# Windowed attention feeding a squared-ReLU FFN on one core: block sums of a batch gathered into one visit, and the scores of a visit's two groups in one run

## The chip, the cores and the metric

The kernel runs on one core of one Trainium2 chip. The metric is device time in microseconds, the median of three runs. Engines are named as in the profile: PE is TensorE (PEld its weight loads), DVE VectorE, ACT ScalarE, POOL GpSimd, SP the queue that issues all DMAs here.

## What is computed

Attention over 4 batches of 8 heads, 768 positions and 64 dimensions, in which a query sees the keys nearer than 16 positions and, besides, one summary of each block of 32 positions: the maximum of the block's keys and the mean of its values. The attention's output, 3072 tokens of 512, goes through a two-layer FFN.

```python
k_sum = k.reshape(B, H, nb, block, D).max(axis=3)      # block = 32, nb = 24
v_sum = v.reshape(B, H, nb, block, D).mean(axis=3)
scores_l = scale * q @ k.T                             # kept where |i - j| < 16
scores_s = scale * q @ k_sum.T + log(block)
a = softmax(concat([masked scores_l, scores_s]))
x = a @ concat([v, v_sum])                             # 3072 x 512
out = relu(x @ w_in) ** 2 @ w_out                      # 512 -> 2048 -> 512
```

## The kernel before

**Groups.** Queries are taken in 48 groups of 64, 12 to a batch, all heads at once. A group sees 118 key columns: 24 block maxima and 94 neighbours. The keys of a batch lie in one SBUF tile `kb`, whose first 24 columns are the block maxima (`batch_k`: loads KL, maxima KM on DVE). So that a group's 118 columns are contiguous, the 24 maxima are copied along `kb` to stand just ahead of the window (`move`, task KC, on POOL).

**Block means of the values** (`batch_v`) are matmuls against a constant matrix: 768 rows of values are loaded in six DMAs (FV), three tasks (VM) of 16 small matmuls each (24x128 outputs) add them up in one PSUM buffer `vps`, and VS copies it to SBUF, from where three groups of each batch fetch it (LS). From batch 1 on the loaded values lie in the three buffers `t`, which the weight conversion and the output copies use too.

**The FFN** works on units of 8 groups (512 tokens) and 16 slices of the inner dimension. FI is 12 matmuls of 128x512 into a PSUM buffer `h`, RL, SQ, GH and GL on ACT and DVE make the squared ReLU in two parts, FO is 12 matmuls of 128x512 (6 each at a unit's first and last slices). Weights are loaded raw (WL) and converted in the first 115 us (WM, WH on ACT, WR, WJ, WW on DVE). There are 2 buffers `h`; FI, the value products and the block means share them.

**A visit** (`visit`, from group 10 on one for each pair of groups) puts attention work between two FFN items of PE. V11 is the visit that multiplies the values of groups 10 and 11 and makes the scores of 12 and 13. Before, `products` emits the 16 score matmuls of the first group, then `move` on POOL, then the 32 value matmuls of the earlier pair, then the 16 score matmuls of the second group, which need what POOL moved. 19 visits, V9 to V45, do all of this; V47 has values alone. Softmax (M, X, E, R, N, T on DVE and ACT) and a transposition through DRAM (TW, TR) lie between a group's scores and its values.

**Order.** `Plan.order` runs a list of tasks through a small model of costs, keys and buffers and so fixes the order of each engine's instructions; each engine then executes in that order. The means' tasks are keyed some 28 us ahead of their batch.

Of the kernel before, what the change touches and what calls it, by code (L numbers as in the profile page):

```python
# [42 lines left out]
ONE_EXP = 1  # L43
NPE = 8
LAG = 2
HALVED = 2


# [4 lines left out]
def first_key(w, S):  # L53
    return min(max(TQ * w - WINDOW + 1, 0), S - LOC)
# [140 lines left out]
def attention_then_relu2_ffn(  # L195
# [75 lines left out]


    places = [f"w{f}" for f in reversed(range(SINGLE, NF))]

    def lend(name, *shapes):
        b = buf(places.pop(0), 1, (P, 4 * DM), F32, f"{name}_lent")
# [145 lines left out]
    t_means = add("means", "POOL", 1.0, make_means, -88)  # L422

    def batch_v(b):
        key = wanted(b * NW) - 28 if b else -60
        out_ps = h_buf(f"vps{b}")
        vs = vs_bufs[b] = buf("vs", 1, (NB, DM), F32, f"vs{b}")
        last = None
        for i in range(0, S // P, 2):
            if b:  # L430
                x = buf("t", 3, (P, 2 * DM), F32, f"fv{b}_{i}")
                xs = [Part(x, 0, DM), Part(x, DM, 2 * DM)]
            else:
                x, xs = first_v[i], first_v[i : i + 2]
            loads = []
            for k in range(2):
                new = not k and (b or i % 4 == 0)
                loads.append(add(
                    f"FV{b}_{i + k}", "SP", 0.45,
                    lambda i=i + k, x=xs[k]: nc.sync.dma_start(out=x.tile, in_=vS[b, i * P : (i + 1) * P, :]),  # L440
                    key - 4 + i + k, behind=None if new else t, take=[x] * bool(new), use=[x] * (not new),
                    size=4 * P * DM, begin=key - 10 if b else 0, late=LATE if b else 0,
                ))
# [15 lines left out]

        def gather():  # L460
            for c in range(NSQ):
                copy(out=vs.tile[:, c * P : (c + 1) * P], in_=out_ps.tile[c * SQ : c * SQ + NB, :P])

        copy = nc.scalar.copy if b else nc.vector.tensor_copy
        t_VS[b] = [add(f"VS{b}", "ACT" if b else "DVE", 1.1, gather, key + 7, [last], take=[vs], use=[out_ps])]


    t_QL, s_bufs = {}, {}
# [1 line left out]
    def loads(g):  # L470

        b, w = divmod(g, NW)
        k0 = first_key(w, S)
        due = wanted(g)
        q, vv = q_bufs[g], v_bufs[g]
        early = g < EARLY
        lq = t_QL[g] = add(
            f"QL{g}", "SP", 0.45, lambda: nc.sync.dma_start(out=q.tile, in_=qW[g]), due - (26 if early else 50), take=[q],
            size=2 * P * DM, begin=due - (45 if early else 65),
        )  # L480

        def load_v():
            if g < vF.shape[0]:

                nc.sync.dma_start(out=vv.tile, in_=vF[g])
                return

            for r0, r1 in ((0, 96),) if k0 + 96 <= S else ((0, 64), (64, LOC)):
                nc.sync.dma_start(out=vv.tile[NB + r0 : NB + r1, :], in_=vS[b, k0 + r0 : k0 + r1, :])

        def load_s():
            nc.sync.dma_start(out=vv.tile[:NB, :], in_=vs_bufs[b].tile)  # L492

        def copy_s():
            nc.gpsimd.tensor_copy(out=vv.tile[:NB, :], in_=vs_bufs[b].tile)
# [5 lines left out]
        if g < EARLY or w < NV or (b == 0 and g < EARLY + NV):  # L501
            ts = t_VS[b]
            if g >= COPIED:
                key = FIRST_LS + g if early else due - 19
                lv.append(add(f"LS{g}", "SP", 0.45, load_s, key, ts + lv, use=[vv, vs_bufs[b]], size=4 * NB * DM))
            else:
                lv.append(add(f"LS{g}", "POOL", 0.62, copy_s, due - 8, ts + lv, use=[vv, vs_bufs[b]]))

    def mask_of(g):
        w = g % NW  # L510
        off = first_key(w, S) - TQ * w
        return masks[off], t_mask[off]
# [26 lines left out]

    def move(g):  # L540

        k0, nxt = (first_key(w, S) for w in (g % NW, g % NW + 1))
        nc.gpsimd.tensor_copy(out=kb[:, :, nxt : nxt + NB], in_=kb[:, :, k0 : k0 + NB])  # L543

    def keys_of(g, pairs):

# [3 lines left out]
    def first_attention(g):  # L550


        loads(g)
        due = wanted(g)
        parts = [(0, 1), (2, 3)] if g == 0 else [range(NPAIR)]
        by_pe = g < PE_MASKS
        s_bufs[g] = [o_buf(f"s{g}_{i}") for i in range(len(parts))]
        t_S[g] = []
        for i, pairs in enumerate(parts):
            t_S[g].append(add(  # L560
                f"S{g}_{i}", "PE", (1.1 if by_pe else 0.6) / len(parts), lambda i=i, pairs=pairs: scores(g, pairs, by_pe, i),
                due - 15, keys_of(g, pairs) + [t_unscale, mask_of(g)[1]] * by_pe, take=[s_bufs[g][i]], use=[q_bufs[g]],
            ))
        softmax(g, by_pe)
# [160 lines left out]
                    rhs=av[:KEYS, 2 * c : 2 * c + 2, j, :], start=True, stop=True,  # L725
                )

    def visit(both, then=()):

        n, g = len(both), both[-1]  # L730
        due = wanted(g)
# [7 lines left out]
        use = [a_bufs[g] for g in both] + [v_bufs[g] for g in both]  # L739
        if g >= RING:  # L740
            deps.append(t_FI[(g - RING) // UG, NF - 1])
        if then:
            s = s_buf(f"s{then[0]}")
            for g in then:
                loads(g)
                s_bufs[g] = [s]
            deps += keys_of(then[0], range(NPAIR)) + [t_QL[then[1]]] + [t_T[g] for g in both]
            use += [q_bufs[g] for g in then]
# [11 lines left out]
        t_v = add(  # L760
            f"V{both[-1]}", "PE", 0.65 * n + 0.6 * len(then), products, due, deps, take=[x_ps] + [s] * bool(s), use=use
        )
# [210 lines left out]
    def groups(n):  # L973

        nonlocal done_g
        while done_g < n:
            g = done_g
            if g and g % NW == 0:
                batch_k(g // NW)
                batch_v(g // NW)  # L980
            if g < FIRST_S:
                first_attention(g)
                if g < UG:
                    visit([g])
                done_g += 1
            else:
                visit([g - 2, g - 1], [g, g + 1])
# [79 lines left out]
```

## Time and profile before

| | |
|---|---|
| median of 3 runs | 621.16 us (620.18 to 621.87) |
| the profiled execution | 620.11 us, its span 618.4 us |
| PE busy | 606.0 us, 98% of the span |
| DVE, ACT, POOL busy | 321.3, 268.8, 25.7 us |
| chain that ended last | PE 88%, DMA 7% |
| granted PE clock | 1.000 |

The span runs from the first to the last instruction; the 1.7 us between it and the execution's time lie around it. Busy is summed time of an engine's instructions. The chain is followed back from the last instruction, at each step to what released it.

### The profile page before, as it was taken

To read this page: it belongs to the slowest core of one execution; us is meant where nothing else is said; L and a number is where in the kernel's file an instruction comes from. 1 tells how busy PE (TensorE), PEld (TensorE's weight loads), DVE (VectorE), ACT (ScalarE), POOL (GpSimd) and SP (SyncE) were. 2 spreads that over 40 slices of the span, in tenths; PEclk is the share of its full clock that TensorE was granted. 3 is DMA by queue.
4 is the path that set the end of the run, shared out by engine and by line. 5 is a ranking of instruction groups with operands and counts; after the bars stand their busy time and mean duration, and the time that the engine had idled before them with its cause. 6 is when DMAs were issued, how large, how long until landed. Compare 5 with 4: busy or idle time off the path is not lost.

```text
span 618.4 us, 11030 instructions
## 1 busy us (share of the span) xinstructions
PE 606.0 (98%) x4252; PEld 494.5 (80%) x4252; DVE 321.3 (52%) x601; ACT 268.8 (43%) x708; POOL 25.7 (4%) x86
## 2 busy tenths in 40 slices
PE   8889999999999999999999999999999999999997
PEld 7777778888888788888888788888888888888885
DVE  5999998753353533543652764535445442322221
ACT  2997697744454443442432533323343322322221
POOL 4200010000000000000000000000000000000000
PEclk9999999999999999999999999999999999999999
DMA  8998995234325631222314642232323020100001
GB/s 319 307 359 304 346 313 178 79 91 144 90 78 170 205 96 69 77 78 69 111 55 160 203 131 68 61 93 70 102 78 103 14 69 1 68 1 0 1 1 68
DMA packets 56015, 74.66 MB, mean 121 GB/s; under 512 B 6548, under 2 KB 33172, under 8 KB 55964
## 3 DMA queue, kind: packets, MB, share of 16 engines
q1 hardware_dynamic: 55964, 73.97, 37.4%
q8 instruction: 33, 0.54, 0.4%
q14 instruction: 18, 0.15, 0.1%
HBM read 56.28 MB, written 16.78 MB: 118 GB/s over the span
## 4 chain that ended last, share of the span: by engine, by line
PE 88%; DMA 7%; SPq 2%; DVE 1%; issue 1%; POOL 0%; ACT 0%; POOLq 0%
PE h L886 40%; PE o L919 38%; PE att L919 4%; DMA raw<-wW 3%; PE att L533 3%; PE x L722 3%; DMA qvpa_lent<-vF 2%; DMA fv_lent<-vS 1%; PE vps L450 1%; DMA turn<-a 0%; POOL kb L543 0%; DMA v<-vS 0%; DVE w L840 0%; SPq L492 0%; SPq L820 0%
## 5 line engine op out<-in xcount | busy, mean ns | idle before, releaser
L886 PE MATMUL h<-xh,w 128*128 128x512 f32 x752 | 233.0, 391 | 0.1
L919 PE MATMUL o<-w,gh 128*128 128x512 f32 x688 | 177.9, 392 | 0.6 <-ACT os L957 0.6
L886 PEld LDWEIGHTS h<-xh,w 128*128 128x128 f32 x752 | 140.5, 188 | 30.9 <-issue 0.9
L919 PEld LDWEIGHTS o<-w,gh 128*128 128x128 f32 x688 | 128.0, 188 | 29.3 <-issue 2.4
L886 PE MATMUL h<-xl,w 128*128 128x512 f32 x376 | 146.3, 389 | 0.0
L895 ACT ACTIVATE r<-h 128x512 f32<-128x512 f32 x94 | 55.9, 595 | 198.1 <-PE h L886 198.0
L901 DVE TENSOR_TENSOR r<-r 128x512 f32<-128x512 f32 x64 | 44.1, 690 | 140.3 <-ACT r L895 140.2
L906 DVE TENSOR_TENSOR gl<-r,gh 128x512 fp32r<-128x512 f32 x94 | 64.9, 690 | 96.7 <-ACT gh L903 65.3
L919 PE MATMUL o<-w,gl 128*128 128x512 f32 x344 | 98.0, 389 | 0.0
L903 ACT CAST gh<-r 128x512 fp32r<-128x512 f32 x94 | 58.3, 620 | 56.2 <-DVE r L901 28.1
L886 PEld LDWEIGHTS h<-xl,w 128*128 128x128 f32 x376 | 70.6, 188 | 14.7
L647 ACT ACTIVATE p<-p,nm 128x118 f32<-128x118 f32 x160 | 60.9, 383 | 34.2 <-DVE nm L611 34.2
L919 PEld LDWEIGHTS o<-w,gl 128*128 128x128 f32 x344 | 64.6, 188 | 13.5
L595 DVE SCALAR_TENSOR_TENSOR p<-att,mask 128x236 f32<-128x236 f32 x76 | 26.9, 395 | 20.5 <-PE att L533 20.5
L543 POOL COPY kb<-kb 128x96 f32<-128x96 f32 x44 | 18.0, 409 | 460.0 <-PE att L533 413.0
L647 ACT ACTIVATION_READ_ACCUMULATOR p<-p,nm 128x1 f32 x160 | 30.0, 188 | 0.0
L695 DVE STREAM_TRANSPOSE a<-p 128x512 f32<-128x512 f32 x40 | 28.3, 707 | 0.7
L666 DVE TENSOR_TENSOR p<-p,nm 128x472 f32<-128x472 f32 x40 | 26.0, 649 | 1.1
L611 DVE TENSOR_REDUCE nm<-p 128x4 f32<-128x472 f32 x40 | 25.5, 638 | 0.6
L533 PE MATMUL att<-kb,q 64*64 64x118 f32 x608 | 24.1, 274 | 0.8 <-POOL kb L543 0.8
L774 ACT CAST xh<-x 128x512 fp32r<-128x512 f32 x20 | 11.7, 584 | 26.5 <-PE x L722 26.5
L722 PE MATMUL x<-a,v 118*64 118x64 f32 x640 | 23.0, 225 | 0.0
(117 smaller groups left out, 410.2 us busy)
## 6 DMA issues: line engine op xcount, KB each, us to landing
raw<-wW SPq DMA_DIRECT2D x32, 512.0 KB, 6.5
turn<-a SPq DMA_DIRECT2D x160, 64.0 KB, 1.8
a<-turn SPq DMA_DIRECT2D x40, 256.0 KB, 2.5
v<-vS SPq DMA_DIRECT2D x33, 192.0 KB, 3.5
kb<-kT SPq DMA_DIRECT2D x16, 384.0 KB, 5.2
out<-os SPq DMA_DIRECT2D x24, 256.0 KB, 2.1
q<-qW SPq DMA_DIRECT2D x40, 128.0 KB, 2.8
fv<-vS SPq DMA_DIRECT2D x18, 256.0 KB, 4.9
```

Source lines behind the costliest of these rows:

```text
L533: nc.tensor.matmul(score_at(g, part, j)[c * TQ : (c + 1) * TQ, :], lhsT=q_bufs[g].tile[rows, p, :] if term else unscale[rows, :], rhs=kb[r ...
L595: nc.vector.scalar_tensor_tensor(out=pr.tile[:, j, :KEYS], in0=x, scalar=SCALE, in1=mask_of(g)[0].unsqueeze(1).broadcast_to([P, x.shape[1] ...
L647: nc.scalar.activation(x, score_tile(g, p % parts)[:, p] if by_pe else x, AF.Exp, bias=nm.tile[:, p : p + 1], scale=SCALE if by_pe else 1. ...
L666: nc.vector.tensor_tensor(out=x, in0=x, in1=nm.tile[:, 2 * NPAIR : 3 * NPAIR].unsqueeze(2).broadcast_to([P, NPAIR, KEYS]), op=ALU.mult)
L695: nc.vector.transpose(out=a.tile.rearrange("p (j n r) -> p j n r", j=NSQ, n=NPAIR), in_=pr.tile.rearrange("p n (j c) -> p j n c", c=SQ),)
L722: nc.tensor.matmul(x_of(i)[h % 2 * D : (h % 2 + 1) * D, h // 2, :], lhsT=v_bufs[g].tile[:KEYS, h * D : (h + 1) * D], rhs=av[:KEYS, 2 * c : ...
L886: nc.tensor.matmul(cut(h), lhsT=lhs.tile[:, k * P : (k + 1) * P], rhs=rhs[:, k, c0 : c0 + n], start=(i == 0), stop=(i == 3 * KT - 1),)
L895: t2 = add(f"RL{name}", "ACT", act, lambda: nc.scalar.activation(cut(r), cut(h), AF.Relu), due + 3, [t1], take=[r], use=[h])
L901: lambda: nc.vector.tensor_tensor(out=cut(r), in0=cut(r), in1=cut(r), op=ALU.mult), due + 4, [t2], use=[r],
L903: t4 = add(f"GH{name}", "ACT", act, lambda: nc.scalar.copy(out=cut(gh), in_=cut(r)), due + 5, [t3], take=[gh], use=[r])
L906: lambda: nc.vector.tensor_tensor(out=cut(gl), in0=cut(r), in1=cut(gh).bitcast(F32), op=ALU.subtract),
L919: nc.tensor.matmul(o_of(o, t), lhsT=terms[i][0].tile[:, (t - t0) * P : (t - t0 + 1) * P], rhs=terms[i][1].tile, start=(first and i == 0), ...
```

## The change

Four things change. The 48 matmuls of a batch's means, for batches 1 to 3, become part of one visit (the one ahead of the batch: V11, V23, V35), ahead of its scores. A visit's scores of both groups stand together, ahead of its values. The second group no longer reads `kb`: ACT copies its 118 columns into a tile `kw` beforehand (`window`, task KW, two copies of 128x4x24 and 128x4x94 elements, 19 times), and POOL's move of an even group falls away. Buffers: batch 1's values are loaded into the places of the weights w15 and w14, lent before to the first batch, and the means of batches 2 and 3 lie in a `t` buffer. The keys of the FV loads move, and the first half of unit 0 is keyed 1 us earlier.

```diff
+FV_LEAD, FV1_LEAD = 2.0, 17.0
...
+    LENT_AGAIN = places[:2]
...
-    HALF_AT = 27.0, 33.0
+    HALF_AT = 26.0, 33.0
...
     def batch_v(b):
-        key = wanted(b * NW) - 28 if b else -60
+        key = wanted(b * NW - 1) - (FV_LEAD if b > 1 else FV1_LEAD) if b else -60
...
+        if b == 1:
+
+            again = [Buf(kinds[p], (P, 4 * DM), F32, f"fv{b}_{p}") for p in LENT_AGAIN]
+            later_v = [Part(x, j * DM, (j + 1) * DM) for x in again for j in range(4)]
...
+            vs = Part(buf("t", 3, (P, 2 * DM), F32, f"vs{b}"), 0, DM)
...
+            mms.append(mm)
+            all_loads += loads
+            all_x.append(x)
+            if b:
+                continue
...
+        if b:
+            return all_loads + [t_means], out_ps, all_x, mms, done
...
-                            rhs=kb[rows, p, k0 : k0 + KEYS] if term else mask_of(g)[0][rows, :],
+                                else windows[g].tile[rows, p, :] if g in windows else kb[rows, p, k0 : k0 + KEYS]
...
-        k0, nxt = (first_key(w, S) for w in (g % NW, g % NW + 1))
+        k0, nxt = (first_key(w, S) for w in (g % NW - (g >= FIRST_S), g % NW + 1))
...
+    def window(g):
+
+        x = windows[g] = buf("kw", 1, (P, NPAIR, KEYS), F32, f"kw{g}")
+        old, k0 = (first_key(w, S) for w in (g % NW - 1, g % NW))
+
+        def copy():
+            nc.scalar.copy(out=x.tile[:, :, :NB], in_=kb[:, :, old : old + NB])
+            nc.scalar.copy(out=x.tile[:, :, NB:], in_=kb[:, :, k0 + NB : k0 + KEYS])
+
+        return add(f"KW{g}", "ACT", 0.75, copy, wanted(g - 2) + 3, keys_of(g - 1, range(NPAIR))[1:], take=[x])
...
         def products():
-            if then:
-                scores(then[0], range(NPAIR), False)
-                move(then[0])
+            if block_sums:
+                for mm in mms:
+                    mm()
+            for g in then:
+                scores(g, range(NPAIR), False)
             values(both, x_of)
-            if then:
-                scores(then[1], range(NPAIR), False)
```

On PE, this is V11 before, between FI and FO items of unit 0 (att0 and att1 are the score tiles, q12 and q13 the groups' queries, x11 the values' PSUM tile; the other score rows alternate between att0 and att1):

```order
L886 MATMUL h0_8_1234<-xh_70,w8_1166 128x512 x2
L886 MATMUL h0_8_1234<-xl_71,w8_1166 128x512
L533 MATMUL att0_66<-kb_69,q12_702 64x118
L533 MATMUL att1_67<-kb_69,q12_702 64x118
...
L722 MATMUL x11_1254<-a10_1079,v2_82 64x64 x8
L722 MATMUL x11_1254<-a11_1139,v0_80 64x64 x8
L533 MATMUL att0_66<-kb_69,q13_1020 64x118
L533 MATMUL att1_67<-kb_69,q13_1020 64x118
...
L886 MATMUL h0_9_1305<-xh_70,w9_1225 128x512 x2
```

And this is V11 now:

```order
L945 MATMUL h0_9_1230<-xl_71,w9_1201 128x512
L465 MATMUL vps1_1251<-fv1_w15_933,means_85 24x128 x16
L465 MATMUL vps1_1251<-fv1_w14_957,means_85 24x128 x8
L564 MATMUL att0_66<-kb_69,q12_716 64x118
L564 MATMUL att1_67<-kb_69,q12_716 64x118
...
L564 MATMUL att0_66<-kw13_1126,q13_1026 64x118
L564 MATMUL att1_67<-kw13_1126,q13_1026 64x118
...
L769 MATMUL x11_1250<-a10_1091,v2_82 64x64 x8
L769 MATMUL x11_1250<-a11_1146,v0_80 64x64 x8
L978 MATMUL o0_0_790<-w7_1024,gh0_7_1181 128x512 x4
```

The means of batch 1 stand at the head of V11, both score groups follow in one run, and the values come last; an FI item that stood behind V11 (h0_9) now stands ahead of it, so that 7 FFN items in place of 8 lie between V11 and V13. Where the means of batch 1 stood before on PE, in three places among unit 0's items (vps1 their PSUM tile):

```order
L886 MATMUL h0_5_1006<-xl_71,w5_938 128x512
L450 MATMUL vps1_1036<-fv1_0_911,means_85 24x128 x8
L919 MATMUL o0_0_795<-w3_840,gh0_3_933 128x512 x4
...
L919 MATMUL o0_1_861<-w3_840,gl0_3_936 128x512 x2
L450 MATMUL vps1_1036<-fv1_2_963,means_85 24x128 x8
L886 MATMUL h0_6_1099<-xh_70,w6_960 128x512 x2
...
L919 MATMUL o0_1_861<-w5_938,gl0_5_1143 128x512 x2
L450 MATMUL vps1_1036<-fv1_4_1064,means_85 24x128 x8
L919 MATMUL o0_0_795<-w6_960,gh0_6_1151 128x512 x4
```

All three places are gone now. For batch 2 the first two of them stood around V23's own rows and the third one item later; for batch 3 all three stood right behind V33; now they head V23 and V35.

On ACT, behind V11, now (vps1 to SBUF is VS1, `xh` the values' high part, kw15 the window of group 15, p0 the first of the two softmaxes):

```order
L962 CAST gh0_9_1319<-r0_9_1309 128x512
L896 CAST w12_1323<-t12_1311 128x2x512
L482 COPY fv1_w14_957<-vps1_1251 24x128 x4
L833 CAST xh_70<-x11_1250 128x4x128
L587 COPY kw15_1353<-kb_69 128x4x24
L588 COPY kw15_1353<-kb_69 128x4x94
L694 ACTIVATE p0_83,nm0_77<-p0_83,nm0_77 128x118 x4
```

Before, the cast of `xh` stood there without a copy of the means ahead of it and without the two window copies behind it. On SP, where batch 1's values are loaded, before (raw7 to raw10 are weights, turn and a the transposition, q and v loads of groups, kb the batch's keys):

```order
L820 DMA raw7_891<-wW 128x512 x2
L440 DMA fv1_0_911<-vS 128x512
L712 DMA a9_850<-turn9_856 128x512
L440 DMA fv1_0_911<-vS 128x512
L820 DMA raw8_940<-wW 128x512 x2
L440 DMA fv1_2_963<-vS 128x512 x2
...
L393 DMA kb_69<-kT 128x768 x4
...
L440 DMA fv1_4_1064<-vS 128x512 x2
L820 DMA raw9_1072<-wW 128x512 x2
```

and now:

```order
L879 DMA raw7_897<-wW 128x512 x2
L759 DMA a9_868<-turn9_886 128x512
L455 DMA fv1_w15_933<-vS 128x512 x4
L455 DMA fv1_w14_957<-vS 128x512 x2
L879 DMA raw8_963<-wW 128x512 x2
...
L395 DMA kb_69<-kT 128x768 x4
...
L879 DMA raw9_1062<-wW 128x512 x2
```

All six value loads stand ahead of the weights raw8 and of the keys now, where two of them did before.

## Rows read from the trace of the kernel before

**Rows 1.** The page, busy time, share of the span and instructions of each engine.

```profile
PE 606.0 (98%) x4252; PEld 494.5 (80%) x4252; DVE 321.3 (52%) x601; ACT 268.8 (43%) x708; POOL 25.7 (4%) x86
```

**Rows 2.** Chain that ended last: start us, us, work; around V19 and V47.

```profile
190.76 2.72 PE h L886 x12
195.69 2.94 PE o L919 x12
...
506.74 2.72 PE o L919 x12
509.46 1.08 PE x L722 x32
510.54 2.94 PE h L886 x12
```

**Rows 3.** Timeline of PE, the second scores of V19 and what follows.

```profile
195.06 0.63 PE L533 MATMUL att<-kb,q 64*64 64x118 f32 x16
195.62 0.73 PE L919 MATMUL o<-w,gh 128*128 128x512 f32 x2
```

**Rows 4.** Timeline of PE at 25 us: score-shaped runs that follow each other.

```profile
25.14 0.41 PE L533 MATMUL s<-mask,unscale 64*64 64x118 f32 x8
25.34 0.41 PE L533 MATMUL s<-kb,qvpa_lent 64*64 64x118 f32 x8
```

**Rows 5.** Chain that ended last, around the means of batches 1 and 2.

```profile
61.21 2.96 PE h L886 x12
...
64.80 2.95 PE o L919 x12
...
68.32 3.01 PE h L886 x12
...
209.52 2.72 PE h L886 x12
215.58 2.94 PE o L919 x12
219.09 2.99 PE o L919 x12
```

**Rows 6.** Chain that ended last, around V33.

```profile
340.64 2.72 PE h L886 x12
...
347.65 1.65 PE o L919 x6
```

**Rows 7.** Timeline at V33: the means of batch 3.

```profile
345.52 1.51 PE L450 MATMUL vps<-fv,means 128*24 128x128 f32 x48
```

**Rows 8.** Chain that ended last, at V9.

```profile
55.70 2.72 PE o L919 x12
...
59.14 1.39 POOL kb L543
```

**Rows 9.** Timeline of PE: waits at V11's second scores and early in unit 0.

```profile
38.65 0.39 PE L886 MATMUL h_0b<-xl,w 128*128 128x256 f32 x1 [0.66 <-DVE xl L777]
...
87.69 0.64 PE L533 MATMUL att<-kb,q 64*64 64x118 f32 x16 [0.28 <-POOL kb L543]
```

**Rows 10.** Groups by line: busy us, mean ns of one, idle before.

```profile
L957 ACT COPY os<-o 128x512 f32<-128x512 f32 x11 | 6.5, 587 | 9.8 <-DVE os L957 8.1 <-DMA v<-vS 1.4
...
L462 ACT COPY vs<-vps 24x128 f32<-24x128 f32 x12 | 3.1, 256 | 0.7 <-PE vps L450 0.6
```

**Rows 11.** Busy time by stretch: PE, PEld, DVE, ACT, POOL, clock, DMA share, GB/s.

```profile
58.00:92.00 34.00, 33.19 (x290) 25.61 (x289) 31.38 (x47) 25.25 (x49) 2.98 (x3) 1.00 0.97 329
```

**Rows 12.** Timeline of DVE and SP: the weights raw8, and the transposition of group 13.

```profile
62.15 0.70 DVE L826 TENSOR_SCALAR raw<-raw 128x1024 uint32<-128x1024 uint32 x1 [1.76 <-DMA raw<-wW]
...
103.53 0.33 SPq L712 DMA_DIRECT2D a<-turn  x1
```

**Rows 13.** The page's DMA issues: count, size, median us from issue to landing.

```profile
a<-turn SPq DMA_DIRECT2D x40, 256.0 KB, 2.5
```

**Rows 14.** Chain that ended last, the first scores of V13.

```profile
110.31 0.56 PE att L533 x16
```

More of the change, by code (lines that the diff above doesn't have):

```diff
@@ L424, in batch_v @@
     def batch_v(b):
-        key = wanted(b * NW) - 28 if b else -60
+        key = wanted(b * NW - 1) - (FV_LEAD if b > 1 else FV1_LEAD) if b else -60
         out_ps = h_buf(f"vps{b}")
-        vs = vs_bufs[b] = buf("vs", 1, (NB, DM), F32, f"vs{b}")
-        last = None
+        copy = nc.scalar.copy if b else nc.vector.tensor_copy
+        last, all_loads, all_x, mms = None, [], [], []
+        if b == 1:
+            again = [Buf(kinds[p], (P, 4 * DM), F32, f"fv{b}_{p}") for p in LENT_AGAIN]
+            later_v = [Part(x, j * DM, (j + 1) * DM) for x in again for j in range(4)]
+        own = b > 1
+        if own:
+            vs = Part(buf("t", 3, (P, 2 * DM), F32, f"vs{b}"), 0, DM)
+        else:
+            vs = later_v[S // P] if b else first_v[S // P]
+        vs_bufs[b] = vs
         for i in range(0, S // P, 2):
-            if b:
+            if b == 1:
+                x, xs = later_v[i], later_v[i : i + 2]
+            elif b:
                 x = buf("t", 3, (P, 2 * DM), F32, f"fv{b}_{i}")
@@ L436, in batch_v @@
             for k in range(2):
-                new = not k and (b or i % 4 == 0)
+                new = not k and (b > 1 or i % 4 == 0)
                 loads.append(add(
@@ L440, in batch_v @@
                     lambda i=i + k, x=xs[k]: nc.sync.dma_start(out=x.tile, in_=vS[b, i * P : (i + 1) * P, :]),
-                    key - 4 + i + k, behind=None if new else t, take=[x] * bool(new), use=[x] * (not new),
-                    size=4 * P * DM, begin=key - 10 if b else 0, late=LATE if b else 0,
+                    key + (0.1 if b else 1) * (i + k) - 4 * (not b), behind=None if new else t, take=[x] * bool(new), use=[x] * (not new),
+                    size=4 * P * DM, begin=key - 2 if b else 0, late=LATE if b else 0,
                 ))
@@ L461, in gather, with done @@
             for c in range(NSQ):
-                copy(out=vs.tile[:, c * P : (c + 1) * P], in_=out_ps.tile[c * SQ : c * SQ + NB, :P])
-        copy = nc.scalar.copy if b else nc.vector.tensor_copy
-        t_VS[b] = [add(f"VS{b}", "ACT" if b else "DVE", 1.1, gather, key + 7, [last], take=[vs], use=[out_ps])]
+                copy(out=vs.tile[:NB, c * P : (c + 1) * P], in_=out_ps.tile[c * SQ : c * SQ + NB, :P])
+        def done(t):
+            t_VS[b] = [add(
+                f"VS{b}", "ACT" if b else "DVE", 1.1, gather, key + 7 if b == 0 else t.key + 0.4, [t],
+                take=[vs] * own, use=[out_ps] + [vs] * (not own),
+            )]
+        if b:
+            return all_loads + [t_means], out_ps, all_x, mms, done
+        done(last)
     t_QL, s_bufs = {}, {}
@@ L491, in load_s @@
         def load_s():
-            nc.sync.dma_start(out=vv.tile[:NB, :], in_=vs_bufs[b].tile)
+            nc.sync.dma_start(out=vv.tile[:NB, :], in_=vs_bufs[b].tile[:NB])
         def copy_s():
-            nc.gpsimd.tensor_copy(out=vv.tile[:NB, :], in_=vs_bufs[b].tile)
+            nc.gpsimd.tensor_copy(out=vv.tile[:NB, :], in_=vs_bufs[b].tile[:NB])
         lv = t_LV[g] = [
@@ L500, in loads, with means_too @@
         ]
-        if g < EARLY or w < NV or (b == 0 and g < EARLY + NV):
+        def means_too():
+            if not (g < EARLY or w < NV or (b == 0 and g < EARLY + NV)):
+                return
             ts = t_VS[b]
@@ L507, in loads @@
                 lv.append(add(f"LS{g}", "POOL", 0.62, copy_s, due - 8, ts + lv, use=[vv, vs_bufs[b]]))
+        return means_too
     def mask_of(g):
@@ L535, in scores @@
                             lhsT=q_bufs[g].tile[rows, p, :] if term else unscale[rows, :],
-                            rhs=kb[rows, p, k0 : k0 + KEYS] if term else mask_of(g)[0][rows, :],
+                            rhs=(
+                                mask_of(g)[0][rows, :] if not term
+                                else windows[g].tile[rows, p, :] if g in windows else kb[rows, p, k0 : k0 + KEYS]
+                            ),
                             start=term, stop=not (by_pe and term),
@@ L550, in first_attention @@
     def first_attention(g):
-        loads(g)
+        loads(g)()
         due = wanted(g)
@@ L726, in values, with visit @@
                 )
-    def visit(both, then=()):
+    def visit(both, then=(), block_sums=None):
         n, g = len(both), both[-1]
@@ L741, in visit @@
             deps.append(t_FI[(g - RING) // UG, NF - 1])
+        means_too = []
+        take = [x_ps]
+        if block_sums:
+            more, out_ps, x, mms, block_sums_done = block_sums
+            deps += more
+            use += x
+            take.append(out_ps)
         if then:
@@ L744, in visit @@
             for g in then:
-                loads(g)
+                means_too.append(loads(g))
                 s_bufs[g] = [s]
-            deps += keys_of(then[0], range(NPAIR)) + [t_QL[then[1]]] + [t_T[g] for g in both]
-            use += [q_bufs[g] for g in then]
+            deps += keys_of(then[0], range(NPAIR)) + [t_QL[then[1]], window(then[1])] + [t_T[g] for g in both]
+            use += [q_bufs[g] for g in then] + [windows[then[1]]]
             if then[0] == FIRST_S:
@@ L752, in products @@
         def products():
-            if then:
-                scores(then[0], range(NPAIR), False)
-                move(then[0])
+            if block_sums:
+                for mm in mms:
+                    mm()
+            for g in then:
+                scores(g, range(NPAIR), False)
             values(both, x_of)
-            if then:
-                scores(then[1], range(NPAIR), False)
         t_v = add(
-            f"V{both[-1]}", "PE", 0.65 * n + 0.6 * len(then), products, due, deps, take=[x_ps] + [s] * bool(s), use=use
-        )
+            f"V{both[-1]}", "PE", 0.65 * n + 0.52 * len(then) + 1.4 * bool(block_sums), products, due, deps,
+            take=take + [s] * bool(s), use=use,
+        )
+        if block_sums:
+            block_sums_done(t_v)
+        for f in means_too:
+            f()
         for g in then:
@@ L977, in groups @@
             g = done_g
+            sums = None
             if g and g % NW == 0:
                 batch_k(g // NW)
-                batch_v(g // NW)
+                sums = batch_v(g // NW)
             if g < FIRST_S:
@@ L986, in groups @@
             else:
-                visit([g - 2, g - 1], [g, g + 1])
+                visit([g - 2, g - 1], [g, g + 1], sums)
                 softmax(g)
```

1 line of the change is left out of this document (added).

## The prediction

> **What bounds the kernel now.** The page's busy times come first: PE is busy for 98% of the span, no other engine for more than 52% [rows 1]. The chain of waits comes next, because it shows what PE's time is made of: FFN items of 12 wide matmuls follow each other at 2.72 us, and only around attention work does the distance grow. So the kernel's time is the items (fixed by this change) plus what the visits and the means add, plus the places where PE waits. I price each by one subtraction: from the modelled end of the item ahead to that of the item behind, less that item's own 2.72 us. An ordinary visit: 195.69 + 2.94 - (190.76 + 2.72) - 2.72 = 2.43 us [rows 2]. V47, values alone: 510.54 + 2.94 - (506.74 + 2.72) - 2.72 = 1.30 us [rows 2].
>
> **1. Both groups' scores in one run.** In the visit the second scores start at 195.06 and the next wide item at 195.62, so a run of 16 score matmuls costs 0.56 us with the change of shape at its end [rows 3]. What 16 more cost inside a run is shown early on, where score-shaped runs of 8 follow each other with 0.20 us from start to start, and no gap: 0.40 us for 16 [rows 4]. So a visit falls by 0.56 - 0.40 = 0.16 us. The same follows from V47: values alone 1.30, a run ahead of them 0.56, 16 more matmuls 0.40, together 2.26 against 2.43. There are 19 such visits: **-3.0 us**. Bounds: nothing, if one group's scores after the other's cost a full 0.56; and 19 x 0.18 = 3.4 us, since the rows are rounded to 0.01 at both ends of each difference.
>
> The Trainium skill (page "TensorEngine Tiling (Array Packing)", section "Key Properties") says that a change of tiling mode drains the engine. By it each visit has three changes in place of four; with an isolated run of means (0.84 us below, 16 matmuls of some 0.025 in it) split over its two changes, one costs 0.22 us and the 19 visits would give 4.2 us instead of 3.0. The rows price the one change that is removed, so I stay with them.
>
> **2. The means in three visits.** Before, batch 1's three runs stand alone: 64.80 + 2.95 - (61.21 + 2.96) - 2.72 = 0.86, and 68.32 + 3.01 - (64.80 + 2.95) - 2.72 = 0.86 [rows 5]; the third I take as 0.84. Batch 2: V23 with two runs next to it takes 215.58 + 2.94 - (209.52 + 2.72) - 2.72 = 3.56, so 1.13 over a visit, and the third, alone, 219.09 + 2.99 - (215.58 + 2.94) - 2.72 = 0.84 [rows 5]. Batch 3: from the end of the item ahead of V33 to the end of the half item (6 matmuls, 1.36) behind it, 347.65 + 1.65 - (340.64 + 2.72) - 1.36 = 4.58 us, or 2.15 over a visit [rows 6]. Here all 48 matmuls stand in one run, from 345.52 to a last start near 346.76; with the 0.19 us by which a run of scores exceeds its matmuls' starts PE would have gone on at 346.95, and did at 347.65 [rows 6, 7]. So the run costs 1.45 and 0.70 is a wait: the output buffers of the unit that had ended could not be emptied, since the three buffers `t` held batch 3's values. Now those values are loaded after that unit's output is stored, and this wait has no successor that I see. Sum before 2.56 + 1.97 + 2.15 = 6.68; now three runs of 1.45, 4.35: **-2.3 us**. Bounds: -1.6 if a wait of that kind stays, -2.6 if the run next to the scores costs only 1.35.
>
> **3. POOL's move off PE's path.** Within a visit the second scores waited for the move. In steady state it hides beneath the values, but at V9 it took 1.39 us, and the visit cost 61.21 + 2.96 - (55.70 + 2.72) - 2.72 = 3.03, so 0.60 too much [rows 5, 8]; at V11 PE waited 0.28 us [rows 9]. Now the second scores read `kw`, copied a visit ahead: **-0.9 us**. Bounds -0.6 and -1.0.
>
> **4. The copies on ACT.** A copy of 128 elements takes 256 ns and one of 512 elements 587 ns [rows 10]; between them, 96 and 376 elements give some 0.25 and 0.47, or 0.7 us a visit, 14 us in all, on an engine that is 43% busy [rows 1]. From V13 on this hides in ACT's idle time, since nothing on PE needs the result for six items or more. If that cover were gone it would cost up to 0.7 at each of the 19. I take **0**. Queued behind the copies are the exponentials of the two groups; those wait for DVE's maxima at about the same time.
>
> The Trainium skill ("SBUF — State Buffer") adds that GpSimd and some VectorE work lock each other out of a port pair, and that ScalarE has its own. It would explain a move of 1.39 us, and says that `kw` will not be stretched so; no row of ACT's copies of keys exists yet.
>
> **5. The first 115 us.** Here the cover is thin: from 58 to 92 us DVE is busy 31.4 of 34 us and the DMA engines 97% [rows 11]. Three things move.
> - The weights raw8 come behind all six value loads instead of two. DVE already waited 1.76 us for them [rows 12]. Four loads of 256 KB at 329 GB/s are 3.2 us [rows 11]; against it, SP no longer stops for a buffer `t`, and ACT converts w7 earlier. And PE needs w8 earlier: FI8 now stands ahead of FO6, one item of 2.7 us, and has lost the three runs of means ahead of it, 2.6 us. I see 0 to 2.0 us of new waits.
> - V11 takes both buffers `h`, for the means and the values, so FI10, one item (2.72 us) behind it, needs the copy of the means, four copies of 256 ns [rows 10], 1.0 us of ACT's time, which is queued behind a weight cast. 0 to 1 us.
> - Between V11 and V13 one item falls out. Before, the transposition of group 13 landed at 103.53 + 2.5 = 106.0 [rows 12, 13], and V13's values began at 110.31 + 0.56 = 110.9 [rows 14]: 4.9 us spare. Now 2.72 goes with the item, 1.0 and 0.7 may go to ACT's new work ahead of the exponentials, and 0.40 is won since the values now stand behind both scores: 0.9 us spare.
> - Early in unit 0 PE waited 0.66 us for a low part of x [rows 9]; the new keys may shorten this or move it.
> Together I take **+0.5 us**, between -0.7 and +3.
>
> **Sum.** 620.1 (the profiled execution) - 3.0 - 2.3 - 0.9 + 0 + 0.5 = 614.4 us. That execution was 1.0 us below the median of the runs, so the median should be **615.4 us**.
>
> **The rivals.**
> - *The other engines take part of it back* in the first 115 us: weights w8 and w9 late, FI10 late, V13 late, together 2 to 4 us instead of 0.5. For it speaks DVE's and the DMA engines' load [rows 11], against it that PE never waited long there, and that unit 0's total work is unchanged. 617 to 619.3 us.
> - *The scores' run is no cheaper* (the change doesn't do what it is to do on PE): each group's 16 matmuls keep their 0.56 us. For it: no row shows two groups' scores in this order; against it, [rows 4]. Term 1 goes, 618.4 us.
> - *Slower than before*: the softmax between V11 and V13 becomes the path. It had 4.9 us spare and I leave 0.9; each us beyond is a us of PE, and the kernel is slower by over 0.3% once the chain is longer by about 8 us more than I reckon (5.7 us of gain and 1.9 us of margin), say if ACT stands behind a weight cast that waits for raw weights still on their way. Some 623 us or more. Only DVE's load speaks for it.
>
> **How the numbers follow.** 0.3% of 621.16 is 1.9 us, about what this kernel's measurement can tell from no change: faster below 619.3, slower above 623.0. Chances: the forecast (613 to 617) 0.70, the engines' share 0.14, no cheaper run 0.06, slower 0.04, other mishaps that leave about the old time 0.06. All gains at their far bounds and the early wait gone give 621.2 - 3.4 - 2.6 - 1.0 - 0.7 = 613.5; the low end is 613.0, a little below. The high end reaches into the first two rivals, 618.6; beyond it I leave some 0.14, and below 613.0 some 0.05. Faster takes the forecast, the second rival and nearly all of the first: 0.88; same 0.08, slower 0.04.
>
> **What would show it.** A steady visit in the chain near 2.27 us from item to item; V11, V23 and V35 near 3.7; no wait for POOL on PE; no wait behind V33; in the first 115 us no PE wait over 1 us behind FI1. A steady visit at 2.4 would fell term 1; waits for DVE, ACT or DMA at FI8 to FI10 or V13 would be the first rival.

## The result, and the profile after

The changed kernel takes **615.28 us** in the median of four runs (614.49 to 615.65), beside 620.67 us (620.12 to 621.87) for the kernel before on the same chip: a ratio of 0.9901, 95% interval 0.9887 to 0.9916. Two more series gave 614.14 us (ratio 0.9894, 0.9876 to 0.9912) and 614.85 us (0.9904, 0.9874 to 0.9934). Predicted were 615.4 us, between 613.0 and 618.6.

The profiled execution took 614.92 us with a span of 613.2; before, 620.11 and 618.4. The page's busy times, which answer to [rows 1]:

```profile
PE 601.9 (98%) x4252; PEld 495.2 (81%) x4252; DVE 321.7 (52%) x601; ACT 280.6 (46%) x746; POOL 16.9 (3%) x67
```

PE has as many instructions as before and is busy 4.1 us less, with the same share of the span. ACT has 38 more, two for each of 19 visits, and POOL 19 fewer. The change took time out of PE's own path, and the other engines gave little of it back (one wait, below).

Where it went is read in the chain that ended last (start us, us, work): V19, V23 with batch 2's block sums, V33 (its values and the half item behind them), V35 with batch 3's block sums, and V47. These answer to [rows 2] and [rows 5, 6]. (Counted from V13 on in the chain, the visit that [rows 2, 3] call V19 is V21; ordinary visits are alike, and no number hangs on its name.)

```profile
167.64 2.72 PE o L978 x12
170.36 0.97 PE att L564 x32
171.33 1.08 PE x L769 x32
172.41 2.94 PE h L945 x12
...
215.71 2.72 PE o L978 x12
218.43 1.44 PE vps L465 x48
219.87 0.97 PE att L564 x32
220.84 1.08 PE x L769 x32
221.92 2.94 PE o L978 x12
...
342.36 1.08 PE x L769 x32
343.44 1.58 PE o L978 x6
...
364.07 2.72 PE o L978 x12
366.79 1.44 PE vps L465 x48
...
370.28 2.94 PE o L978 x12
...
501.55 2.72 PE o L978 x12
504.27 1.08 PE x L769 x32
505.35 2.94 PE h L945 x12
```

By the prediction's own subtraction the ordinary visit is now 172.41 + 2.94 - (167.64 + 2.72) - 2.72 = 2.27 us. V23 and V35 come out at 221.92 + 2.94 - (215.71 + 2.72) - 2.72 = 3.71 and 3.71; V47 stays at 1.30. The two groups' 32 score products are one piece of 0.97 us (0.56 + 0.41) where there were two pieces of 0.56. Behind V33's values (342.36 + 1.08 = 343.44) the next item starts at once: the wait of 0.70 us of before is gone, as is every wait of a visit for POOL's move.

Two stretches have to be kept apart from here on. From the end of the item ahead of V9 to the span's end, before took 618.4 - 58.42 = 559.98 us [rows 8]. After, the item ahead of V9 ends at 56.41 + 2.72 = 59.13, and 554.07 us remain: **5.9 us less**. The way up to V9 took 0.71 us *more*. The chain at V9, and at FI0_10:

```profile
56.41 2.72 PE h L945 x12
59.13 0.97 PE att L564 x32
60.10 1.11 PE x L769 x32
...
90.47 1.05 ACT w L896
...
92.22 0.27 ACT fv_w L482
92.48 0.04 issue
92.53 3.01 PE h L945 x12
```

V9 has no wait in it. FI0_10 (the last row) waits for the four copies of batch 1's block sums (`fv_w`, L482), and these stood on ACT behind a weight cast (L896). It is the one new wait behind V9.

### The profile page after: what moved, and what is told of

The parts are those of the page before. It is cut to its first block, busy times and chain, and to the rows that moved or that the text cites. A ratio compares the mean times of both kernels' runs of the same rounds, so it can differ in the third digit from the quotient of the medians.

```text
span 613.2 us, 10978 instructions
## 1 busy us (share of the span) xinstructions
PE 601.9 (98%) x4252; PEld 495.2 (81%) x4252; DVE 321.7 (52%) x601; ACT 280.6 (46%) x746; POOL 16.9 (3%) x67
## 4 chain that ended last, share of the span: by engine, by line
PE 87%; DVE 6%; ACT 2%; DMA 2%; issue 1%; SPq 0%; DVEq 0%
PE h L945 39%; PE o L978 37%; PE att L978 4%; PE x L769 3%; PE att L564 3%; DMA kb<-kT 2%; DVE t L891 1%; ACT qvpa_lent L694 1%; DVE kb L398 1%; DVE raw L885 1%; PE vps L465 1%; PE s L564 1%; ACT w L896 1%; DVE w L899 1%; DVE nm L658 0%
## 5 line engine op out<-in xcount | busy, mean ns | idle before, releaser
L769 PEld LDWEIGHTS x<-a,v 118*64 118x64 f32 x640 | 20.3, 138 | 3.3 <-issue 2.4
L899 DVE TENSOR_TENSOR w<-t,w 128x1024 fp32r<-128x1024 f32 (+1 forms) x19 | 19.9, 1049 | 2.1 <-ACT w L896 2.1
```

The lines of the kernel that those rows point to most:

```text
L769: nc.tensor.matmul(x_of(i)[h % 2 * D : (h % 2 + 1) * D, h // 2, :], lhsT=v_bufs[g].tile[:KEYS, h * D : (h + 1) * D], rhs=av[:KEYS, 2 * c : ...
L899: nc.vector.tensor_tensor(out=part(1, w.tile), in0=by_n(temp()), in1=part(0, w.tile).bitcast(F32), op=ALU.subtract)
```

## The experiments

In each profile I read the same two stretches: the time at which the item ahead of V9 ends, and from there to the end.

| kernel | median us | ratio to before (95%) | up to V9 | V9 to the end |
|---|---|---|---|---|
| before | 620.67 | | 58.42 | 559.98 |
| changed | 615.28 | 0.9901 (0.9887 to 0.9916) | 59.13 | 554.07 |
| changed, again | 614.14 | 0.9894 (0.9876 to 0.9912) | 59.93 | 554.27 |
| changed, third | 614.85 | 0.9904 (0.9874 to 0.9934) | 60.54 | 554.06 |
| 1 block sums only | 619.97 | 0.9981 (0.9960 to 1.0003) | 57.69 | 560.61 |
| 2 scores apart | 618.03 | 0.9931 (0.9908 to 0.9955) | 59.60 | 556.80 |
| 3 copies four times | 617.69 | 0.9938 (0.9915 to 0.9961) | 59.06 | 556.34 |
| 4 sums' copy ahead | 614.40 | 0.9882 (0.9862 to 0.9903) | 58.56 | 553.84 |
| 4 sums' copy ahead, again | 613.23 | 0.9882 (0.9860 to 0.9903) | 58.61 | 553.59 |
| 5 no copies | 615.11 | 0.9908 (0.9891 to 0.9925) | 57.34 | 554.56 |
| 6 early key back | 616.29 | 0.9920 (0.9900 to 0.9940) | 56.42 | 555.18 |
| 7 copies on POOL | 623.60 | 1.0049 (1.0031 to 1.0067) | 57.8 | 564.3 |
| 7 the same, longer buffer | 622.85 | 1.0040 (1.0027 to 1.0054) | 58.7 | 563.6 |
| 8 gh and gl shifted | 621.30 | 1.0014 (0.9998 to 1.0030) | 58.31 | 560.39 |

(The last column is the span less the one ahead of it; in experiment 7 both are from the timeline, where V9's scores begin. Each kernel's ratio is to the kernel before on its own chip.)

**1. The block sums alone.** The visit goes back to first scores, POOL's move, values, second scores, and reads the keys' own buffer; the copies go. The main part of the edit:

```diff
...
-            for g in then:
-                scores(g, range(NPAIR), False)
+            if then:
+                scores(then[0], range(NPAIR), False)
+                move(then[0])
             values(both, x_of)
+            if then:
+                scores(then[1], range(NPAIR), False)
...
```

> Changed kernel without its scores part: first group's scores, POOL's move, values, second group's scores, as in the kernel before; only the block sums are in one visit. Theory (terms 2, 3 and 1 add): of the 5.3 us the two later block sums give 1.2, that of V11 some 1.0 more, so about 2.3 less what the first 115 us lose; visits stay at 2.43 us and the visits with block sums take 2.43 + 1.45 = 3.88. Time 618.4 to 619.5 us (ratio 0.996 to 0.998). Rival (the block sums carry most of the gain, the scores' order little): 616 or less. Rival (the block sums' one visit is also what costs the first 115 us their 1.1 us): 619.5 or more, with FI0_10's wait for the means' copy still there.

The median, 619.97, lies just above the first theory's range and in that of the last rival, whose wait is not there; the profile says why. The chain at V23:

```profile
221.50 1.44 PE vps L465 x48
...
225.16 2.94 PE o L965 x12
```

So V23 takes 225.16 + 2.94 - 221.50 - 2.72 = 3.88 us, with 1.44 in the block sums, as expected. There is no wait behind V33, and none at FI0_10, which stands one item later here. From the end of the item behind V9 on, 618.3 - (61.94 + 4.54) = 551.8 us remain, where before had 618.4 - (61.21 + 2.96) = 554.2: 2.4 us less, of the 2.6 that the block sums (2.36) and V11's wait (0.28) should give. So the block sums in one visit cost the first 115 us little by themselves. But at V9 the timeline of PE has this:

```profile
58.18 1.15 PE L753 MATMUL x<-a,v 118*64 118x64 f32 x32
61.31 0.64 PE L564 MATMUL att<-kb,q 64*64 64x118 f32 x16 [1.98 <-POOL kb L574]
...
62.72 1.06 PE L932 MATMUL h<-xh,w 128*128 128x512 f32 x2
```

The move took 2.84 us here (1.39 in before's profile; the median of this kernel's 44 moves is 0.27), and behind the wait the wide products run at half pace. The same stretch by windows (the seventh column is the granted clock):

```profile
58.00:62.00 4.00, 2.02 (x61) 1.57 (x54) 3.13 (x4) 3.22 (x6) 2.84 (x1) 1.00 1.04 415
62.00:66.50 4.50, 4.50 (x13) 3.58 (x14) 4.45 (x11) 2.69 (x15) 0.00 (x0) 0.62 1.01 345
```

PE stood for 1.98 us, and over the 4.5 us that follow the granted clock was 0.62 in the mean, between its two levels of 1.2 and 2.4 GHz: the item took 4.54 us in place of 2.94. So this wait cost 2.0 + 1.6 us in this run, where before's profile had 0.51. How many of the twelve runs (617.54 to 623.27 us) paid as much one profile can't tell. The Trainium skill (page "SBUF — State Buffer", section "SBUF: two separate sides") says that VectorE and GpSimd share a port pair by an exclusive lock for a whole instruction; the trace agrees as far as it goes, since VectorE was at work without a gap from 56.43 to 61.13 and the move ended at 61.25, but no run here separates the lock from other causes.

**2. The two groups' scores apart again**, with copied keys, move and order as in the changed kernel.

```diff
-            for g in then:
+            for g in then[:1]:
                 scores(g, range(NPAIR), False)
             values(both, x_of)
+            for g in then[1:]:
+                scores(g, range(NPAIR), False)
```

> Changed kernel with the values' products put back between the two groups' scores; the copied keys, the move and the order of everything else stay. Theory (the gain of 0.16 us a visit is the missing change of shape on TensorE): visits go from 2.27 back to 2.43 us, 19 times, so +3.0 us: 618.3 (ratio to before 0.996). Rival A (the gain came from POOL's move being off the path, not from the order): visits stay at 2.27 and the time at 615.3. Rival B (every change of shape costs alike, 0.22): 2.49 a visit, 619.5.

618.03: the theory. The chain at V19:

```profile
168.57 2.72 PE o L980 x12
171.29 0.56 PE att L564 x16
171.86 1.08 PE x L769 x32
172.94 0.56 PE att L564 x16
173.50 2.94 PE h L947 x12
```

173.50 + 2.94 - (168.57 + 2.72) - 2.72 = 2.43 us, to the hundredth what it was before, although nothing waits for POOL here and the keys come from the copied buffer. Rivals A and B fall: the 0.16 us is the order of the three runs and nothing else. From V9 to the end it takes 2.5 to 2.7 us more than the changed kernel, less than 19 x 0.16 = 3.0, because FI0_10 has no wait here.

**3. The copies four times over.**

```diff
-            nc.scalar.copy(out=x.tile[:, :, :NB], in_=kb[:, :, old : old + NB])
-            nc.scalar.copy(out=x.tile[:, :, NB:], in_=kb[:, :, k0 + NB : k0 + KEYS])
+            for _ in range(4):
+                nc.scalar.copy(out=x.tile[:, :, :NB], in_=kb[:, :, old : old + NB])
+                nc.scalar.copy(out=x.tile[:, :, NB:], in_=kb[:, :, k0 + NB : k0 + KEYS])
```

> Changed kernel with the copies of the second group's keys made four times over into the same buffer: ScalarE gets 3 x 0.75 = 2.2 us more in each of 19 visits, 42 us in all. Theory (the copies are hidden: the keys' buffer is asked for long before its visit, and ScalarE is 46% busy): within 0.3% of 615.3. Rival (the copies stand ahead of FI's squares or the casts of weights in ScalarE's queue, and TensorE waits for these): up to 2.2 a visit in the first 115 us, where ScalarE is 80% busy (4 visits, +2 to +9 us), and little later; a wait of TensorE for gh, w or xh would show it.

The time is the lower edge of the rival's: V9 to the end is 2.1 to 2.3 us longer than in the changed kernel. Behind V9 PE's timeline has a wait of 0.21 us for a weight at 78 us and these two, the second in the middle of V13's values:

```profile
93.50 0.73 PE L946 MATMUL h<-xh,w 128*128 128x512 f32 x2 [0.55 <-ACT fv_w L482]
...
111.01 0.69 PE L770 MATMUL x<-a,v 118*64 118x64 f32 x16
112.66 0.69 PE L770 MATMUL x<-a,v 118*64 118x64 f32 x16 [0.96 <-issue]
```

The added copies stand ahead of the exponentials of V13's groups on ACT. First copy and first exponential, in the changed kernel and here:

```profile
92.98 0.28 ACT L587 COPY kw<-kb 128x96 f32<-128x96 f32 x1
...
93.56 0.39 ACT L694 ACTIVATE p<-p,nm 128x118 f32<-128x118 f32 x1
```

```profile
93.96 0.28 ACT L588 COPY kw<-kb 128x96 f32<-128x96 f32 x1
...
96.29 0.40 ACT L695 ACTIVATE p<-p,nm 128x118 f32<-128x118 f32 x1
```

From the one to the other it is 0.58 us there and 2.33 here: 1.75 more on ACT make V13 wait 0.96. So V13 had some 0.8 us to spare in the changed kernel, an estimate from these rows (the prediction left it 0.9). From V13's end to the span's end both kernels take the same (615.4 - 113.35 = 502.05 against 613.2 - 111.19 = 502.01): the sixteen visits there hide four times the copies in full.

**4. The block sums' copy ahead of the cast.** One exchange in ACT's queue: the copy behind V11 is put ahead of weight 12's cast.

```diff
-        for t in plan.order():
+        tasks = plan.order()
+        at = {t.name: i for i, t in enumerate(tasks)}
+        tasks.insert(at["WH12"], tasks.pop(at["VS1"]))
+        for t in tasks:
```

> Changed kernel with one exchange in ScalarE's queue: the copy of batch 1's block sums stands ahead of weight 12's cast, for which ScalarE sat idle 0.55 us waiting for VectorE, rather than behind it. Theory (that copy frees the bank on which FI0_10 waits): the wait of 0.73 us at FI0_10 goes, and the time with it: 614.7 to 614.9 (ratio to the changed kernel 0.999). Rival (the cast is as late as the copy was, and FI0_12 or FO0_12 waits for weight 12 instead): 615.3 to 616, no change.

ACT's timeline:

```profile
89.87 1.06 ACT L482 COPY fv_w<-vps 24x128 f32<-24x128 f32 x4
90.84 1.05 ACT L896 CAST w<-t 128x1024 fp32r<-128x1024 f32 x1
```

The copy uses the time in which ACT had waited for VectorE; the cast begins 0.37 us later than in the changed kernel's profile (90.84 against 90.47, with V11 itself 0.31 earlier), and nothing waits for it. FI0_10 has no wait, V9 to the end takes 553.84 us. It was run once more beside the changed kernel:

> The exchange in ScalarE's queue (the copy of batch 1's block sums ahead of weight 12's cast), beside the changed kernel on one chip. Theory: 0.4 to 0.7 us less than the changed kernel, no wait at FI0_10. Rival (what the first 59 us take from run to run covers it): no difference between the two medians.

> The changed kernel, as the other side for the three kernels beside it: 614 to 615.7, from V9's start to the end 554.1 to 554.4 us as in its two earlier profiles, with a wait of 0.4 to 0.7 at FI0_10, and the way to V9 anywhere between 58.5 and 60.

613.23 us (612.33 to 614.14) against 614.85 (612.95 to 616.97), V9 to the end 553.59 against 554.06. The wait is gone both times and the stretch is 0.2 to 0.7 us shorter than in the three profiles of the changed kernel. At the place itself, on PE's timeline from the start of V11's block sums to the FO item behind FI0_10, those three take 9.57, 9.74 and 9.57 us and these two 9.06 and 9.07: the wait cost 0.5 to 0.7 us. The medians' 1.6 us are more than that; between the two profiled runs (613.89 and 616.36 us) the rest lies ahead of V9. This is the best kernel of the study by its median, by a margin that the intervals do not separate.

**5. No copies.** Order and buffers stay; the second group's scores read the keys' own buffer, so this kernel leaves out the right block maxima for every second group.

```diff
-                                else windows[g].tile[rows, p, :] if g in windows else kb[rows, p, k0 : k0 + KEYS]
+                                else kb[rows, p, k0 : k0 + KEYS]
...
         def copy():
-            nc.scalar.copy(out=x.tile[:, :, :NB], in_=kb[:, :, old : old + NB])
-            nc.scalar.copy(out=x.tile[:, :, NB:], in_=kb[:, :, k0 + NB : k0 + KEYS])
+            pass
```

> Changed kernel without the copies; the second group's scores read the keys' own buffer, where the moved block maxima are not in place yet, so every second group's attention to the block keys is that of wrong keys. Theory (the copies are hidden in full): same time as the changed kernel, 614.5 to 616. Rival (they already push the softmax or a cast onto the path somewhere in the first 115 us): 0.5 to 1.5 less, with the wait of FI0_10 or that at 49.5 us shorter.

615.11 us, beside 614.14 for the changed kernel on the same chip; V9 to the end 554.56 against 554.27. Nothing was to be had: the copies cost nothing that these runs can tell.

**6. The early key back.** `HALF_AT = 26.0, 33.0` becomes `27.0, 33.0`, which moves FO0_1a, FI0_9 and FI0_10 among others.

> Changed kernel with the key of the first half items back at 27.0. Theory (the earlier key is worth little either way): within 1 us of the changed kernel, 614.5 to 616.3. Rival A (the earlier key is what costs the first 59 us their 0.7 us): V9's visit 0.7 earlier in the program's work, 614.6 or less. Rival B (it was needed: weights and low parts come late again): waits for VectorE's w or xl of over 1 us, 616.5 or more.

616.29 against 614.14, with intervals of the ratios that overlap (0.9900 to 0.9940 and 0.9876 to 0.9912). Its profile came to V9 earlier (56.42) and lost some of that behind it (a wait of 1.3 us for a weight's low part at 76 us). Undecided: the medians speak for the earlier key by 2.2 us, while the profiled run of this kernel, at 613.27, was its fastest.

**The changed kernel again**, for the way to V9.

> The changed kernel itself once more, for the noise of the first 59 us: the profiled runs of four kernels with the same order of instructions reached V9 at 58.56 to 59.60 us, and two of them had TensorE at half clock for about 4 us after a wait of 1.6 to 1.8 us at 33 us. Theory (that is chance of the run, not of the change): V9 at 58.5 to 60, everything from V13's end on 502.0 us, time 614.5 to 616. Rival (the changed order itself makes TensorE's first scores late and its start slow): again a late key load, a wait for VectorE's block maxima of over 1 us near 10 us and V9 at 59.1 or later.

V9 came at 59.93, which theory and rival had both allowed; what tells them apart is the late key load of the first profile (PE waited 1.2 us for VectorE's block maxima near 10 us), and it did not come back. All twelve profiles of kernels with this order of PE up to V9 came there between 57.34 and 60.54, the same kernel between 59.13 and 60.54; before's one profile, 58.42, lies among them.

**7. The copies on POOL.**

```diff
-            nc.scalar.copy(out=x.tile[:, :, :NB], in_=kb[:, :, old : old + NB])
-            nc.scalar.copy(out=x.tile[:, :, NB:], in_=kb[:, :, k0 + NB : k0 + KEYS])
+            nc.gpsimd.tensor_copy(out=x.tile[:, :, :NB], in_=kb[:, :, old : old + NB])
+            nc.gpsimd.tensor_copy(out=x.tile[:, :, NB:], in_=kb[:, :, k0 + NB : k0 + KEYS])
...
-        return add(f"KW{g}", "ACT", 0.75, copy, wanted(g - 2) + 3, keys_of(g - 1, range(NPAIR))[1:], take=[x])
+        return add(f"KW{g}", "POOL", 1.6, copy, wanted(g - 2) + 3, keys_of(g - 1, range(NPAIR))[1:], take=[x])
```

> Changed kernel with the copies of the second group's keys made by GpSimd in place of ScalarE. From the move's rows (128x96 in 0.365 us) four to five times as many columns take 1.8 us when nothing disturbs, and up to 2.84 us for 128x96 alone was seen beside a busy VectorE. Theory (the copies have most of a visit's distance to spare on any engine): time within 0.3% of the changed kernel, ScalarE 280 to 266 us busy, GpSimd 17 to 50. Rival (beside a VectorE that is busy without a break GpSimd's copies stretch many times over): KW11 or KW13 take 5 us and more, TensorE waits for kw at V9, V11 or V13, +1 to +5.

623.60 us: slower than before, and for neither reason. The copies were quick (rows of `kw`: duration min/median/max in ns) and PE waited for none of them:

```profile
L587 POOL COPY kw<-kb x19: 268/269/609, 35.3 to 466.2; 128x96 f32<-128x96 f32 x19
L588 POOL COPY kw<-kb x19: 498/505/985, 35.6 to 466.4; 128x376 f32<-128x376 f32 x19
```

What had become slower were FO's products: twelve took 2.81 us in place of 2.72, from start to end of the kernel, at a granted clock of 1.000. The 94 such items make 8.5 of the 10.0 us by which V9 to the end is longer than in the changed kernel; for the rest FI0_10 waits 0.86 us in place of 0.37, and FI items take 2.73 to 2.81. PE's program is the same, row for row, but in this kernel the copies' buffer is taken earlier, so it lies ahead of the buffers gh and gl, and by the compiled program these begin at 212,576 and 222,816 bytes of a partition in place of 210,688 and 220,928: 32 over a multiple of 64. So the same kernel was run with a copies' buffer of 1,920 bytes in place of 1,888.

> The kernel with the copies on GpSimd once more, with the copies' buffer 8 columns longer (1920 bytes a partition in place of 1888), of which nothing is read; same order of instructions. The 8.5 us that it lost lay in FO's products alone (2.81 us for twelve in place of 2.72, at full granted clock and without a wait), and its buffers of gh and gl stood at addresses that are 32 over a multiple of 64, since the copies' buffer is placed ahead of them. Theory (the place of gh and gl in SBUF costs it): FO back at 2.72, time 613.5 to 616. Rival (GpSimd's copies disturb TensorE's reads): FO stays at 2.81 and the time at 622 to 624.

622.85: the theory in this form falls. FO takes 2.80 us, with gh at 212,608 and gl at 222,848 bytes, both 128 over a multiple of 256.

**8. gh and gl shifted in the changed kernel**, with the copies on ACT as they were: gh's buffers are 4 columns longer, of which nothing is read.

```diff
-            buf(tag, nb, (P, TU), dt, f"{tag}{name}") for tag, nb, dt in (("r", 2, F32), ("gh", 3, F32R), ("gl", 3, F32R))
+            buf(tag, nb, (P, TU + 4 * (tag == "gh")), dt, f"{tag}{name}") for tag, nb, dt in (("r", 2, F32), ("gh", 3, F32R), ("gl", 3, F32R))
```

> Changed kernel, copies on ScalarE as they were, with each of gh's three buffers 16 bytes longer, which the allocator makes 32: the first and third gh stay at multiples of 64 bytes, the second gh and all three gl stand 32 over. Same order of instructions. Theory (a stationary operand 32 bytes off costs 7.5 ns a product): FO's products with gl at 396 ns and a third of those with gh, the others 389; 94 items x 12 x 7.5 ns x (4 + 8/3)/12 = 4.7 us, time 619 to 620.5. Rival (place is not the cause): 614 to 616, all of FO at 389.

621.30 us, 6.4 more than the changed kernel beside it, with the same instructions in the same order. In the chain:

```profile
156.69 2.79 PE o L978 x12
159.49 2.75 PE h L945 x12
162.23 2.75 PE o L978 x12
164.98 2.72 PE h L945 x12
167.70 2.79 PE o L978 x12
```

So the place of gh and gl alone costs as much as the whole change gains. My rule was wrong in detail. FO falls into two kinds, 2.79 twice and 2.75 once in a round of the three gh buffers. With the program's order of products laid beside the trace, products start 228 ns apart in the mean with the first gh as stationary operand (the one that PEld loads; it begins at a multiple of 256 bytes), 233 with the second (32 over) and the third (64 over), and 232 with gl (96 over); in the changed kernel it is 227 for all. All kernels that ran at 2.72, before and changed alike, had every gh and gl at a multiple of 256 bytes.

That the stationary operand has to begin at such a multiple does not follow, though. In experiment 7's second kernel one weight, w5, also lies 128 over a multiple of 256. Its FI and FO items of unit 1, and the FO behind them, in the chain:

```profile
161.25 2.79 PE h L945 x12
...
177.37 2.73 PE o L978 x12
...
182.83 2.80 PE o L978 x12
```

The FI item, where w5 is the stationary operand and the moving one (xh, xl) begins at a multiple of 256, is slow. The FO item, where w5 is the moving operand and gh and gl lie 128 over as it does, has its old pace; the next FO, whose weight lies at a multiple of 256, is slow again. So the places of both operands count, and not that of gh and gl alone. Equal places are no full rule either: in the first kernel of experiment 7, where w5, gh and gl are all 96 over, the same FO item takes 2.78. No run tried the places one by one, and the cause stays open. Two more things stay open: why the FI item behind a slow FO takes 2.75 as well, though its operands did not move, and whether POOL's copying adds anything of its own in the two kernels of experiment 7.

## Why the prediction was right

**Term 1, the scores in one run (-3.0): right.** The visit fell from 2.43 to 2.27 us, as [rows 3, 4] had it, and experiment 2 gave exactly 2.43 back with the order alone. The other price, 0.22 for a change of shape by an even split of an isolated run, would have made 4.2; the change that was removed cost 0.16.

**Term 2, the block sums (-2.3): right.** The three runs of 48 take 1.44 us each, in the changed kernel and in experiment 1, 4.32 in place of 6.68: -2.36. The wait behind V33 is gone, with the block sums alone too (experiment 1); that it came from the buffers `t` is argued and was not tried.

**Term 3, the move off the path (-0.9): right in the profile it was read from; as a mean not known.** It removed the 0.60 us at V9 and 0.28 at V11 of that execution. Experiment 1 shows the same wait at 1.98 us, with 1.6 more for the clock behind it. If the kernel before pays that often, the term was too small; one profile of it can't tell.

**Term 4, the copies (0): right.** Leaving them out gains nothing (experiment 5), four times as many cost 2.1 us, all of it up to V13 (experiment 3). They take 0.28 + 0.51 us by their rows; the reckoning said 0.25 + 0.47.

**Term 5, the first 115 us (+0.5): the mechanism partly right, the size not settled.** Named beforehand and found: FI0_10 behind the sums' copy, which stood behind a weight cast. It cost 0.5 to 0.7 us at its place (experiment 4), within the 0 to 1 that were allowed. Not found: a wait for raw8, and one at V13, which had some 0.8 us to spare (experiment 3). Terms 1 to 3 make 6.2 us; from V9 on 5.7 to 5.9 came, so term 5 is +0.3 to +0.5 there. What the change does ahead of V9 can't be told: the first pair of profiles had +0.7, but the changed kernel's own way to V9 varied by 1.4 us. So terms 1, 2 and 4 are shown by experiments, and the mechanism is right; that the median fell within 0.1 us of the forecast is luck, as the other two series (614.14 and 614.85) and the way to V9 show.

The first rival (2 to 4 us taken back) would need longer waits than FI0_10's; the second falls with term 1; the third with V13, which did not wait.

## What to carry to other kernels

Price a reordering on a saturated TensorE from item to item in the chain: a run of 16 small products cost 0.56 us by itself and 0.40 behind others of its shape, and that difference was, to a hundredth, what each visit gained. Copying 1.9 KB a partition ahead on an engine with room, to break a dependency that forced the order, cost nothing that showed and took a wait of 0.3 to 2 us off the path. And when a kernel with an unchanged TensorE program is slower throughout, look at the single product's duration and at where its operands lie, before looking for a wait.

## What the runs showed of the hardware that was not expected

- Where the two operands of a wide product lie in SBUF changes its pace: 2.72 us for twelve against 2.75 to 2.81 with gh and gl moved, 6 to 8 us in the kernel (experiments 7 and 8).
- A wait of TensorE can cost more than itself. Behind 1.98 us of waiting in experiment 1 the granted clock was 0.62 over 4.5 us. The third run of the changed kernel shows it too (windows, columns as above), behind a wait of 2.03 us that ended at 35.25:

```profile
32.00:35.00 3.00, 0.90 (x7) 0.48 (x5) 3.00 (x7) 2.40 (x5) 0.00 (x0) 0.95 1.03 357
35.00:38.00 3.00, 2.75 (x48) 2.52 (x48) 1.31 (x5) 1.59 (x6) 0.00 (x0) 0.50 1.01 368
38.00:41.00 3.00, 3.00 (x21) 2.85 (x14) 2.96 (x7) 3.00 (x11) 0.41 (x1) 0.50 0.97 370
```

For six us TensorE ran at 1.2 in place of 2.4 GHz, and this run came to V9 last of all, at 60.54. Behind waits of 1.83 and 1.59 us at about the same place in experiments 2 and 3 the granted clock was 0.67 to 0.76 over the same six us. A wait of 1.75 us there in before's profile was not followed by a fall, nor were 1.68 us in the second kernel of experiment 7 and 1.56 in the changed kernel's second run. So part of what varies from run to run ahead of V9 is whether the clock falls there.
